# A transfer constant shortened in an instruction planner: accumulating transfers reckoned to land sooner, 70 of them instead of 56, key pairs of the half passes changed, order searched anew

## Chip, core and metric

One core of a Trainium2 chip runs the kernel. The metric is the device time of one execution in microseconds (us), the median over several runs. Engines are named as in the profile: PE (TensorE, matrix products), ACT (ScalarE), DVE (VectorE), POOL (GpSimd), SP (SyncE, which here only issues transfers).

## What is computed

A layer norm, an attention block over it with 32 heads of 20 columns, a token-mixing perceptron over a second layer norm, and a gated sum. S is 2048, D 640, F 1536; all inputs are bf16.

```
xn = layernorm(x)                                   # x: (1, 2048, 640)
q, k, v = split(xn @ wqkv)                          # 32 heads, Dh = 20
p = softmax(q k^T * Dh**-0.5)
s = (p v, heads joined) @ wo
h = layernorm(xn)
u = gelu(einsum("bsd,sf->bdf", h, w1) + b1)         # F = 1536
y = einsum("bdf,fs->bds", u, w2) + b2
out = x + s * silu(y^T)
```

## The kernel before

The instructions of all engines are written by a planner in Python, `_Kern.schedule`, that runs once when the kernel is built. It keeps a clock for each engine (`Prog.T`), adds a reckoned cost for each instruction (`Prog._add`), and always emits next what its own clocks and priorities favour. So a constant of the planner changes no single instruction, but the order of nearly all that come after, and with it who waits for whom.

**Units and passes.** The attention scores are made transposed, in units of 128 keys by 512 queries of one head (L1362, PE). Four heads make a group; 8 groups and 4 query blocks give 32 passes of 64 units, 2048 units in all. The last pass is split into two half passes of 256 queries; there a unit joins two key blocks, named by the list `HP`, of 256 queries each.

**Two ways to the exponential.** Most units go to ACT: PE fills three PSUM banks of one of two bank groups, and one ACT call takes three units (128x1536), or two (128x1024) where the third bank was lent to DVE (L1392, into `pt_sb`). The other units go to DVE, always four heads of one key block together, called a quad here. DVE reads each score tile from PSUM, adds a constant and writes 16-bit integers whose bits are a bf16 power of two (L1403, into `dt_sb`, 128x512, four a quad). Then three more variants of the quad are made, each the first plus a constant, in the bits (L1471, "top", 128x2048, SBUF to SBUF); the four variants are summed with scaled copies of the values (`vs_sb`).

**The accumulating transfer.** A variant can also be made without DVE: POOL issues a transfer from a constant table in DRAM (`kc_scratch_dram`) that adds the constant in place to a variant that isn't needed any more (`emit_x`, L1434, 512 KB). Then a top drops out on DVE. `x_ok` decides on it when a quad has two tops: the reckoned transfer queue must be short, and at least `XLEFT` ACT units of the pass must be left. The transfer waits for the reader of the old variant, on PE (product with the values, L1497) and on DVE (a top); the product with the variant that it makes waits for its landing.

**How the planner reckons it.** On POOL's clock a transfer takes `XISSUE`, then `XMOVE` in a queue of its own, and it is taken as landed `XTAIL` later:

```
if eng == "pool" and ceng != "pool":
    self.T[eng] = start + self.XISSUE
    self.xpipe = max(self.xpipe, start + self.XISSUE) + self.XMOVE
    t.fin = self.xpipe + self.XTAIL
```

With 950, 2900 and 5600 ns that is 9.45 us from the issue to the landing. PE products that need the variant are put in PE's order only behind that time.

**The rest.** Products p v go to one PSUM accumulator (L1497, 32-column pieces of PE side by side); the perceptron and the projections are jobs that PE runs between the score groups (L715 and L723, 32-column and 32-row pieces; L700, L813, L1036); fillers on PE (L1514) add zeros to the accumulator where the planner sees a gap. The weights of the perceptron come in pieces by SP (L850: 1024 KB, L857: 768 KB). ACT also does the gelu (L907) and the tanh of the silu (L920). The residual of most rows is added by POOL's transfers as well (L1078).

**What is searched.** `PLAN` has one string for each stretch of 16 units; a digit chooses a value of one planner option of `OPTS` (slack, priorities, `XLEFT`, and so on) for that stretch.

Of the kernel before, what the change touches and what calls it, by code (L numbers as in the profile page):

```python
# [39 lines left out]
class Prog:  # L40
# [4 lines left out]
    LAT = {"pe": 55.0, "act": 55.0, "dve": 55.0, "pool": 80.0, "sp": 60.0}  # L45
    NXL = 4
    DMAX = 1.4
    XISSUE, XMOVE, XTAIL = 950.0, 2900.0, 5600.0
    TAIL = {"pe": 170.0, "act": 118.0, "dve": 82.0, "pool": 60.0, "sp": 0.0}

    def __init__(self, nc, n_lanes=8):
# [232 lines left out]
class _Kern:  # L284
# [58 lines left out]
    XLEFT, XQ = 20, 4000.0  # L343
# [20 lines left out]
        ("GROT", (1, 0)),  # L364
        ("JOBF", (4, 0, 8)),
        ("EVJ", (36.0, 19.0, 45.0)),
        ("XLEFT", (20, 14, 28, 99)),
        ("XLEFT2", (99,)),
        
        ("NLIVE", (4, 5, 6)),  # L370
        ("D_GUARD", (8, 16, 24)),
    )
    PLAN = (
        "00000000000000000000", "00000000000000000000", "00000000000000000000", "00003000000000000000", "01004000000000000000", "00003000000000000000",
        "00202000000000000000", "00020100000000000000", "10000400000000000000", "00000000000000000000", "00000000001000000000", "00000000000000000000",
        "00000000000000000000", "21004100000000200000", "20100000000000100000", "00000000000000000000", "00000000000000000000", "00204000000000000000",
        "00003000000000000000", "00000000000000000000", "01200000000000000000", "02000030000000000000", "00000000000000000000", "00000000000000000000",
        "00000030000100100000", "00000030000100100000", "01200000000000000000", "02000030000000000000", "10000400000000000000", "20100000000000100000",
        "00003000000000000000", "00000000000000000000", "01000000000000000000", "00000000000000000000", "01000000000000000000", "00000000000000000000",
        "00000000000000000000", "00000000000000000000", "00000000000000000000", "00000000000000100000", "00003000000000000000", "00000000000000000000",  # L380
        "01200000000000000000", "20000000000000000000", "10000000000000000000", "00000000000000000000", "01200000000000000000", "00003000000000000000",
        "00000000000000000000", "00000000000000000000", "10000000000000000000", "10000000000000000000", "00004000001000000000", "00000000000000000000",
        "20020100000000000000", "00000030000100100000", "01003100000000200000", "00000400000000000000", "20000000000000000000", "00000000000000000000",
        "00000000000000000000", "00000000000000000000", "00000000000000000000", "20000000000000000000", "00000000000000000000", "00000000000000000000",
        "00000000000000000000", "02000030000000000000", "20020100000000000000", "00000000000000000000", "00000000000000000000", "00000000000000000000",
        "00000000000000000000", "10000000000000000000", "00000000000000000000", "00000030000100100000", "00000000000000000000", "00000030000100100000",
        "00000000000000000000", "00000000000000000000", "00000000000020000000", "12000000001000000000", "00003000000000000000", "00202000000000000000",
        "00000000000000000000", "00202000000000000000", "00000030000100100000", "00000000000000000000", "20020100000000000000", "00000000000000000000",
        "02000030000000000000", "00000000000000000000", "01003100000000200000", "00000000000000000000", "20020100000000000000", "12000000001000000000",
        "20100000000000100000", "00202000000000000000", "20100000000000100000", "12000000001000000000", "00000030000100100000", "01000000000000000000",  # L390
        "02000030000000000000", "00000000000000000000", "00003000000000000000", "00000000000000000000", "00000000000000000000", "00000000000000000000",
        "01200000000000000000", "00000000000000000000", "00000000000000000000", "01000000000000000000", "00002000000000000000", "00000000000000000000",
        "10000000000000000000", "10000000000000000000", "00000400000000000000", "00000000000000000000", "00020100000000000000", "00000000000000000000",
        "00002000000000000000", "00120100000000100000", "00003000000000000000", "00003000000000000000", "00000000000000000000", "00003000000000000000",
        "00000000000000000000", "00003000000000000000",
    )
    PARTS = (1,)
    DX = (1, 2, 3)
# [78 lines left out]
    def schedule(self):  # L477
# [459 lines left out]
        UP = NB * GH  # L937
        NALL = NG * NTB * UP
        HALF = {NP - 2: 0, NP - 1: 1}
        HP = ((0, 1), (3, 4), (6, 7), (9, 10), (12, 13), (14, 15), (2, 5), (8, 11))  # L940
        units, dunits = [], []
        for q, (G, p) in enumerate(passes):
            if q in HALF:
                a = 256 * HALF[q]
                units.append([[(c0, p * 512 + a, 256, 0, a), (c1, p * 512 + a, 256, 256, a)] for c0, c1 in HP])
                dunits.append([(6, (0, 1)), (7, (2, 3))])
# [1407 lines left out]
```

## Time and profile before

| what | value |
|---|---|
| runs, median (lowest to highest of 3) | 741.89 us (740.93 to 741.89) |
| profiled execution, its own time | 740.37 us |
| its span, first to last instruction | 738.6 us |
| mean granted clock of PE | 0.999 |
| ACT busy | 716.4 us, 97% |
| DVE busy | 705.3 us, 95% |
| PE busy (ends modelled) | 709.1 us, 96% |
| POOL busy | 79.9 us, 11% |

The 1.8 us between the span and the profiled execution's own time lie around the instructions. Three engines are busy for nearly the whole span, so the shares alone don't tell which of them sets the time; the chain of waits and the idle time in front of each group do. In a row of the groups stand line, engine, operation, tiles and shapes, the count, then busy time in us and the mean duration of one in ns, then the engine's idle time in front of them and what ended it. On ACT and DVE instructions overlap: the next one starts some 0.1 to 0.2 us before the last has ended, so the busy time per call is less than the mean duration.

### The profile page before, as it was taken

The numbers are of one execution on the slowest core, as the hardware profiler recorded it, in microseconds if no ns is written. First come the engines' busy times: TensorE is split into PE (matmuls) and PEld (weight loads), VectorE is DVE, ScalarE is ACT, GpSimd is POOL, SyncE is SP. The second block draws the span as 40 slices with busy tenths as digits, with TensorE's granted clock in tenths as the row PEclk, the third lists the DMA queues.
The fourth block names the chain that finished last, engine by engine and source line by source line (L and its number), as shares of the span: only waits on it lengthen the run. The fifth ranks groups of instructions, "written<-read, shape, count | busy, mean of one in ns | idle before, by whom it ended". The sixth has DMA issues, their size and how long they took to land.

```text
span 738.6 us, 23733 instructions
## 1 busy us (share of the span) xinstructions
PE 709.1 (96%) x10544; PEld 237.8 (32%) x10544; DVE 705.3 (95%) x1293; ACT 716.4 (97%) x710; POOL 79.9 (11%) x93
## 2 busy tenths in 40 slices
PE   8899999999999999999999999999999999999997
PEld 6332222222232232322322323232333333233333
DVE  8889999999999999999999999899999999999998
ACT  5999999999999999999999999999999999999995
POOL 4300101010000110000111100111000100121210
PEclk9999999999999999999999999999999999999999
DMA  9768545331444444342644416653368773454333
GB/s 239 146 132 109 103 95 103 69 61 39 95 93 70 84 86 87 80 97 42 146 84 73 80 20 155 125 114 76 83 138 121 116 139 89 88 123 94 63 83 90
DMA packets 132075, 72.56 MB, mean 98 GB/s; under 512 B 84340, under 2 KB 123636, under 8 KB 131924
## 3 DMA queue, kind: packets, MB, share of 16 engines
q1 hardware_dynamic: 122180, 39.71, 25.5%
q0 software_dynamic: 9792, 31.33, 23.6%
q8 instruction: 82, 1.34, 0.8%
q14 instruction: 21, 0.17, 0.1%
HBM read 41.05 MB, written 10.75 MB: 70 GB/s over the span
## 4 chain that ended last, share of the span: by engine, by line
ACT 80%; PE 15%; DVE 2%; DMA 1%; issue 0%; SPq 0%
ACT pt_sb L1392 78%; PE ps_all L1362 5%; PE ps_all L1497 5%; PE ps_all L715 4%; PE ps_all L1036 1%; ACT regB L907 1%; ACT zt_sb L920 1%; DMA regA<-in_A_x_dram 1%; DMA xnT_sb<-regC 1%; DVE dt_sb L1403 1%; DVE dt_sb L1471 0%; DVE bst_sb L596 0%; SPq L541 0%; DVE bst_sb L598 0%; DVE regC L614 0%
## 5 line engine op out<-in xcount | busy, mean ns | idle before, releaser
L1392 ACT ACTIVATE pt_sb<-ps_all 128x1024 bf16<-128x1024 f32 (+1 forms) x681 | 692.8, 1212 | 5.6 <-PE ps_all L1362 4.1
L1403 DVE TENSOR_SCALAR dt_sb<-ps_all 128x512 uint16<-128x512 f32 x536 | 356.1, 683 | 19.3 <-PE ps_all L1362 13.9
L1362 PE MATMUL ps_all<-qk_sb 32*128 32x512 bf16 (+1 forms) x2128 | 268.6, 376 | 17.3 <-ACT pt_sb L1392 15.2
L1471 DVE TENSOR_SCALAR dt_sb<-dt_sb 128x2048 uint16<-128x2048 uint16 x346 | 228.0, 689 | 1.3
L1362 PEld LDWEIGHTS ps_all<-qk_sb 32*128 32x128 bf16 x2128 | 67.9, 91 | 275.4 <-ACT pt_sb L1392 218.2
L1497 PE MATMUL ps_all<-dt_sb,vs_sb 128*21 128x512 bf16 (+1 forms) x1656 | 143.7, 377 | 0.7 <-DVE dt_sb L1471 0.4
L1497 PE MATMUL ps_all<-pt_sb,v_sb 128*21 128x512 bf16 (+1 forms) x1576 | 121.4, 373 | 1.1 <-DVE v_sb L1190 0.8
L1434 POOL DMA_DIRECT2D dt_sb<-kc_scratch_dram x56 | 53.3, 952 | 584.0 <-DVE dt_sb L1471 235.3
L715 PE MATMUL ps_all<-regB,regA 128*32 128x512 bf16 (+1 forms) x1468 | 69.4, 297 | 1.6 <-issue 1.5
L715 PE MATMUL ps_all<-regC,regA 128*32 128x128 bf16 (+1 forms) x1432 | 70.2, 295 | 0.0
L1497 PEld LDWEIGHTS ps_all<-dt_sb,vs_sb 128*21 128x21 bf16 x1656 | 35.8, 90 | 56.3 <-issue 35.9
L1497 PE MATMUL ps_all<-dt_sb,v_sb 128*21 128x512 bf16 (+1 forms) x552 | 52.8, 377 | 0.7 <-DVE tr_sb L1625 0.7
L715 PE MATMUL ps_all<-xnT_sb,wqk_sb 128*32 128x512 bf16 x640 | 48.0, 382 | 0.0
L1497 PEld LDWEIGHTS ps_all<-pt_sb,v_sb 128*21 128x21 bf16 x1576 | 29.2, 90 | 43.3 <-issue 33.4
L723 PE MATMUL ps_all<-regC,regA 32*128 32x512 bf16 x104 | 40.0, 385 | 0.0
L715 PEld LDWEIGHTS ps_all<-regB,regA 128*32 128x32 bf16 x1468 | 29.3, 96 | 25.2 <-issue 13.8
L715 PEld LDWEIGHTS ps_all<-regC,regA 128*32 128x32 bf16 x1432 | 27.6, 96 | 21.2 <-issue 12.7
L1036 PE MATMUL ps_all<-wv_sb,xnT_sb 128*128 128x512 bf16 (+1 forms) x160 | 27.7, 301 | 0.0
L723 PE MATMUL ps_all<-regB,regA 32*128 32x512 bf16 x68 | 26.1, 384 | 0.0
L715 PE MATMUL ps_all<-wv_sb,xnT_sb 128*32 128x480 bf16 x320 | 22.9, 369 | 0.0
L1625 DVE STREAM_TRANSPOSE tr_sb<-ps_all 128x512 f32<-128x512 f32 x31 | 22.0, 710 | 0.0
L1497 PEld LDWEIGHTS ps_all<-dt_sb,v_sb 128*21 128x21 bf16 x552 | 13.9, 90 | 20.9 <-issue 15.8
(88 smaller groups left out, 344.3 us busy)
## 6 DMA issues: line engine op xcount, KB each, us to landing
dt_sb<-kc_scratch_dram POOLq DMA_DIRECT2D x56, 512.0 KB, 6.1
regA<-in_B_w_dram SPq DMA_DIRECT2D x6, 1024.0 KB
regA<-in_B_w_dram SPq DMA_DIRECT2D x8, 768.0 KB
qk_sb<-qk_scratch_dram SPq DMA_DIRECT2D x56, 80.0 KB
qk_scratch_dram<-qs_sb SPq DMA_DIRECT2D x32, 128.0 KB
regA<-in_A_x_dram SPq DMA_DIRECT2D x3, 640.0 KB
ok_scratch_dram<-on_sb SPq DMA_DIRECT2D x96, 20.0 KB
regC<-in_A_x_dram POOLq DMA_DIRECT2D x12, 160.0 KB, 4.1
```

What stands on the lines that cost most here:

```text
L715: fns.append(lambda e, c=c, e_=e_: e.matmul(oc(c, e_), lhsT[:, c:e_], rhs, start=start, stop=stop, tile_position=(0, c)))
L723: row = lambda g: (lambda e: e.matmul(oc(0, 128), lhsT[32 * g:32 * g + 32, :], rhs[32 * g:32 * g + 32, :], start=False, stop=False, tile_p ...
L907: steps.append(("act", lambda e, d=d: e.activation(d, d, AF.Gelu_apprx_tanh), [S_(f"u{f}_{q}") for f in range(f0, f0 + 3) for q in (0, 1)] ...
L920: steps.append(("act", lambda e: e.activation(tt_, z, AF.Tanh), sz, [stt], f"th2_{j}", ac(n)))
L1036: steps.append(("pe", lambda e, c=c: e.matmul(ap, oT_sb[:, c, b * 128:(b + 1) * 128], wo_ap[:, c, c0:c0 + n], start=(opens and c == 0), st ...
L1362: t = pr.pe(lambda e, outp=outp, lhsT=lhsT, rhs=rhs, g=g: e.matmul(outp, lhsT, rhs, start=True, stop=True, tile_position=(32 * g, 0)), rea ...
L1392: tk = pr.act(lambda e: e.activation(outp, inp, AF.Exp, scale=math.log(2.0) / 128.0), reads=[bank_slot[b] for b in banks[:n]], writes=[S_( ...
L1403: tk = pr.dve(lambda e: e.tensor_scalar(w, src, WOFF, 0.0, ALU.add, ALU.max), reads=[bank_slot[bk]], writes=[S_(f"dt{d['tl'][0]}_{g}")], n ...
L1434: t = pr.xdma(lambda e: e.dma_start(dst, src, accum_op=ALU.add), [S_(f"kc{i}")] + sl_, sl_, f"dX{d['q']}_{d['c']}_{k1}")
L1471: tk = pr.dve(lambda e: e.tensor_scalar(dst, src, dk, None, ALU.add), reads=[S_(f"dt{b}_{g}") for b in inb for g in range(4)], writes=[S_( ...
L1497: pr.pe(lambda e: e.matmul(outp, lhsT, rhs, start=(k == 0), stop=last, tile_position=(0, 32 * g)), reads=reads, writes=[bank_slot[AB]], na ...
L1625: steps.append(("dve", lambda e: e.transpose(tr_sb[:, :], ps(AB)), [bank_slot[AB]], [S_("tr")], f"epT{q}", 632.0))
```

## The change

Four edits:

- `XTAIL` goes from 5600 to 4200 ns, so a transfer is taken to land 8.05 us after its issue, not 9.45 us.
- `XLEFT` gets a new first value: 16 units left in the pass are enough for a transfer, where it was 20.
- In the half passes the pairs of key blocks in `HP` change. The two pairs that go to DVE are its last two; they were (2, 5) and (8, 11) and are (1, 4) and (7, 10), which are the first four of the key blocks `RC` of which scaled values exist. The shapes stay.
- `PLAN` is a new table, searched with the new constant.

```diff
-    XISSUE, XMOVE, XTAIL = 950.0, 2900.0, 5600.0
+    XISSUE, XMOVE, XTAIL = 950.0, 2900.0, 4200.0
...
-        ("XLEFT", (20, 14, 28, 99)),
+        ("XLEFT", (16, 20, 14, 28, 99)),
...
     PLAN = (
-        "00000000000000000000", "00000000000000000000", "00000000000000000000", "00003000000000000000", ...
+        "00000000000000000000", "00000000000000000000", "00000000000000000000", "00000000000000000000", ...
...
-        HP = ((0, 1), (3, 4), (6, 7), (9, 10), (12, 13), (14, 15), (2, 5), (8, 11))
+        HP = ((0, 2), (3, 5), (6, 8), (9, 11), (12, 13), (14, 15), (1, 4), (7, 10))
```

What this makes of the instructions, counted in the order of both programs:

| engine, line | before | now |
|---|---|---|
| ACT L1392, two units (128x1024) | 531 | 536 |
| ACT L1392, three units (128x1536) | 150 | 145 |
| ACT L1392, one unit (128x512) | 0 | 1 |
| DVE L1403 (128x512) | 536 | 540 |
| DVE L1471 (128x2048) | 346 | 335 |
| POOL L1434, accumulating transfers | 56 | 70 |
| PE L1497 on `dt_sb`, 512 wide | 2080 | 2096 |
| PE L1497 on `pt_sb`, 512 wide | 1448 | 1444 |
| PE L1514, fillers | 112 | 76 |
| PE L715 / L723 on `regB` (512 wide) | 700 / 68 | 696 / 72 |

All other instructions are the same in kind and number. Up to the first score groups the order is the same on every engine; behind that nearly all rows of PE, ACT and DVE stand otherwise.

POOL's whole queue behind the start, as a piece of the difference (`kc_scratch_dram` is the table of constants; L1078 are the residual's transfers, L1802 clears a weight tile):

```order
-L1434 DMA dt_sb<-kc_scratch_dram 128x2048 x39
+L1434 DMA dt_sb<-kc_scratch_dram 128x2048 x49
 L1802 MEMSET wqk_sb 128x640
-L1434 DMA dt_sb<-kc_scratch_dram 128x2048 x15
+L1434 DMA dt_sb<-kc_scratch_dram 128x2048 x18
 L1078 DMA regC<-in_A_x_dram 128x640 x2
 L1434 DMA dt_sb<-kc_scratch_dram 128x2048
 L1078 DMA regC<-in_A_x_dram 128x640 x4
-L1434 DMA dt_sb<-kc_scratch_dram 128x2048
+L1434 DMA dt_sb<-kc_scratch_dram 128x2048 x2
 L1078 DMA regC<-in_A_x_dram 128x640 x6
```

The added transfers lie in the whole of the attention, ten of them ahead of the clearing of the weight tile, and one among the residual's.

The end of ACT's order before, the last exponentials:

```order
L1392 ACTIVATE pt_sb<-ps_all 128x1536 x2
L1392 ACTIVATE pt_sb<-ps_all 128x1024 x2
L1392 ACTIVATE pt_sb<-ps_all 128x1536
L1392 ACTIVATE pt_sb<-ps_all 128x1024 x5
L1392 ACTIVATE pt_sb<-ps_all 128x1536 x2
L1392 ACTIVATE pt_sb<-ps_all 128x1024
L1392 ACTIVATE pt_sb<-ps_all 128x1536 x2
```

and now:

```order
L1392 ACTIVATE pt_sb<-ps_all 128x1536 x2
L1392 ACTIVATE pt_sb<-ps_all 128x1024
L1392 ACTIVATE pt_sb<-ps_all 128x1536
L1392 ACTIVATE pt_sb<-ps_all 128x1024 x6
L1392 ACTIVATE pt_sb<-ps_all 128x1536 x5
L1392 ACTIVATE pt_sb<-ps_all 128x512
```

The last call takes one unit where it took three, behind five calls of three.

PE's order at the same place before, from the last score group to the end of the last products p v (L1362 scores, L1497 products, L1036 and L1041 the output projection):

```order
L1362 MATMUL ps_all<-qk_sb 128x256 x6
L1497 MATMUL ps_all<-pt_sb,v_sb 21x256 x16
L1497 MATMUL ps_all<-dt_sb,v_sb 21x256 x8
L1497 MATMUL ps_all<-dt_sb,vs_sb 21x256 x16
L1036 MATMUL ps_all<-wv_sb,xnT_sb 128x512
L1041 MATMUL ps_all<-wqk_sb,stage_sb 128x512
L1036 MATMUL ps_all<-wv_sb,xnT_sb 128x512
L1497 MATMUL ps_all<-dt_sb,vs_sb 21x256 x8
L1497 MATMUL ps_all<-pt_sb,v_sb 21x256 x16
```

and now:

```order
L1362 MATMUL ps_all<-qk_sb 128x256 x6
L1497 MATMUL ps_all<-dt_sb,vs_sb 21x256 x8
L1497 MATMUL ps_all<-dt_sb,v_sb 21x256 x8
L1497 MATMUL ps_all<-dt_sb,vs_sb 21x256 x16
L1362 MATMUL ps_all<-qk_sb 128x256 x2
L1497 MATMUL ps_all<-dt_sb,vs_sb 21x256 x8
L1497 MATMUL ps_all<-pt_sb,v_sb 21x256 x16
L1036 MATMUL ps_all<-wv_sb,xnT_sb 128x128 x3
L1497 MATMUL ps_all<-pt_sb,v_sb 21x256 x8
```

The last batch of products holds 8 instead of 16, and a batch of 16 stands ahead of it.

DVE's order from its last score tiles to the transpose of the last half pass before (L1403 score tiles, L1471 tops, L1051 the projection's product with the gate, L1617 to L1622 the close of a half pass):

```order
L1403 TENSOR_SCALAR dt_sb<-ps_all 128x512
L1622 STREAM_TRANSPOSE stage_sb<-on_sb 128x256
L1403 TENSOR_SCALAR dt_sb<-ps_all 128x512
L1471 TENSOR_SCALAR dt_sb<-dt_sb 128x2048 x3
L1051 TENSOR_TENSOR regC<-ps_all,regC 128x512
L1403 TENSOR_SCALAR dt_sb<-ps_all 128x512
L1471 TENSOR_SCALAR dt_sb<-dt_sb 128x2048 x3
L1051 TENSOR_TENSOR regC<-ps_all,regC 128x512
L1617 STREAM_TRANSPOSE tr_sb<-ps_all 128x256
```

and now:

```order
L1403 TENSOR_SCALAR dt_sb<-ps_all 128x512
L1622 STREAM_TRANSPOSE stage_sb<-on_sb 128x256
L1471 TENSOR_SCALAR dt_sb<-dt_sb 128x2048 x2
L1051 TENSOR_TENSOR regC<-ps_all,regC 128x512
L1471 TENSOR_SCALAR dt_sb<-dt_sb 128x2048 x4
L1051 TENSOR_TENSOR regC<-ps_all,regC 128x512
L1617 STREAM_TRANSPOSE tr_sb<-ps_all 128x256
```

Six tops now follow the last score tile, where it was three; the last score tile stands 16 units ahead of ACT's last one, where it was 6.

More of the change, by code (lines that the diff above doesn't have):

```diff
@@ L373 @@
     PLAN = (
[L374 to L393, printed above, removed]
@@ L394 @@
-        "00002000000000000000", "00120100000000100000", "00003000000000000000", "00003000000000000000", "00000000000000000000", "00003000000000000000",
-        "00000000000000000000", "00003000000000000000",
+        "00000000000000000000", "00000000000000000000", "00000000000000000000", "00000000000000000000", "40010000000000000000", "00000000000000000000",
+        "10000400000000000000", "10000400000000000000", "00000000000000000000", "01200000000000000000", "00000000001000000000", "00000000000000000000",
@@ new lines @@
+        "00000000000000000000", "00000030000100100000", "01200000000000000000", "00000000000000100000", "00000100000000000000", "01200000000000000000",
+        "00000000000020000000", "00004000001000000000", "00004000000000000000", "00202000000000000000", "12000000001000000000", "00000100000000000000",
+        "20000000000000000000", "00120100000000100000", "01004000000000000000", "00000100000000000000", "20004100000000000000", "00000000000020000000",
+        "20000000000000000000", "02000030000000000000", "00000000000020000000", "00000400000000000000", "12000000001000000000", "20100000000000100000",
@@ new lines @@
+        "00000000000020000000", "00120100000000100000", "00000000000020000000", "00000000000020000000", "00000000000000000000", "20100000000000100000",
+        "00000000000020000000", "00000000000020000000", "00000000000000000000", "00000000000000000000", "00002000000000000000", "00000000000020000000",
+        "01004000000000000000", "02000030000000000000", "20000000000000000000", "20100000000000100000", "20020100000000000000", "20020100000000000000",
+        "00000000000020000000", "01202000000000000000", "20100000000000100000", "01003100000000200000", "01000000000000000000", "20000000000000000000",
@@ new lines @@
+        "20100000000000100000", "01200000000000000000", "00204000000000000000", "00000000001000000000", "20000000000000000000", "00002000000000000000",
+        "00000030000100100000", "00000400000100000000", "02000000000000000000", "00000030000100100000", "01202000000000000000", "00003000000000000000",
+        "00000000000020000000", "01003100000000200000", "20100000000000100000", "00003000000000000000", "20004100000000000000", "00000000001000000000",
+        "20000000000000000000", "00000000000000000000", "02000030000000000000", "00000000000020000000", "20100000000000100000", "00000000000020000000",
@@ new lines @@
+        "00000030000100100000", "00003000000000000000", "01200000000000000000", "10000000000000000000", "00000000000000000000", "00000000000000000000",
+        "00000000000000000000", "00000000001000000000", "00000000000000000000", "02000030000000000000", "20020100000000000000", "01200000000000000000",
+        "10000000000000000000", "00000000000000000000", "02000030000000000000", "00000000000000000000", "00000000000000000000", "00000000000000000000",
+        "00000000000000000000", "00000000000000000000", "00000000000000000000", "00000000000000000000", "00000000000000000000", "12000000001000000000",
@@ new lines @@
+        "40010000000000000000", "00002000000000000000", "02000000000000000000", "00020100000000000000", "20000000000000000000", "02000000000000000000",
+        "00000000000000100000", "01003100000000200000", "00000000000000000000", "10000000000000000000", "10000400000000000000", "01003100000000200000",
+        "00000000000020000000", "00000100000000000000", "00000000000000000000", "00000000001000000000", "00000000000020000000", "01000000000000000000",
+        "20100000000000100000", "00000000000020000000",
```

## Prediction

> **What bounds the kernel now.** I read the page's shares and its chain of waits first, then ACT by stretches, then who waits for whom.
>
> ```profile
> span 738.6 us, 23733 instructions
> PE 709.1 (96%) x10544; PEld 237.8 (32%) x10544; DVE 705.3 (95%) x1293; ACT 716.4 (97%) x710; POOL 79.9 (11%) x93
> ACT 80%; PE 15%; DVE 2%; DMA 1%; issue 0%; SPq 0%
> ...
> core 0: us, ACT busy (x), PEclk, DMA share, GB/s
> 40.10:437.43 397.33, 396.87 (x397) 1.00 0.44 83
> 437.72:729.91 292.19, 289.68 (x282) 1.00 0.54 106
> 729.91:738.60 8.69, 0.00 (x0) 0.95 0.21 75
> ```
>
> Three engines look full, but 80% of the chain is ACT's. The three stretches (length, then ACT's busy time) say it without a chain: from 40.10 us to its last call at 729.91 us ACT idles 0.46 us in the first and 2.51 us in the second. So the span is a start of 40.10 us, ACT's work, about 3.3 us of its idle time (0.29 us between the stretches included) and an end of 8.69 us. DVE and PE matter only where they let ACT wait, or in that end.
>
> ```profile
> PEld ps_all L1362 <- ACT pt_sb L1392: 218.2, 501, 1.5
> ACT pt_sb L1392 <- PE ps_all L1362: 4.1, 6, 1.1
> PE ps_all L715 <- issue: 1.5, 2, 1.2
> ```
>
> PE's weight loads for the scores waited 501 times for ACT to empty a bank, 0.44 us each; ACT waited for scores six times. PE is thus ahead at nearly every score group. The longest wait of ACT, 1.1 us, stands behind a stall of PE of 1.2 us that no semaphore explains.
>
> **The change, part by part.** ACT first, since it makes the sum.
>
> ```profile
> L1392 ACT ACTIVATE pt_sb<-ps_all 128x1024 bf16<-128x1024 f32 (+1 forms) x681 | 692.8, 1212 | 5.6 <-PE ps_all L1362 4.1 <-PE ps_all L1497 0.5 <-PE ps_all L723 0.3
> ...
> L1392 ACT ACTIVATE pt_sb<-ps_all 128x1024 bf16<-128x1024 f32 x531 | 510.2, 1121 | 2.3 <-PE ps_all L1362 1.4 <-PE ps_all L723 0.3
> L1392 ACT ACTIVATE pt_sb<-ps_all 128x1536 bf16<-128x1536 f32 x150 | 223.8, 1534 | 3.3 <-PE ps_all L1362 2.7 <-PE ps_all L1497 0.5
> ...
> L673 ACT ACTIVATE xnT_sb<-ps_all 128x512 bf16<-128x512 bf16 x2 | 1.2, 597 | 0.7 <-PE ps_all L666 0.6
> ```
>
> Five calls of three units become calls of two: 1534 - 1121 = 413 ns each, 2.07 us less. One call of one unit is new. Calls overlap by 1212 - 692.8/681 = 195 ns; a 128x512 call of 597 ns (L673) so costs 0.40 us, and 1121 - 413 - 195 gives 0.51. I take 0.45, in the middle. **ACT: -1.6 us**, between -1.56 and -1.67, and it lies on the path at full size, because ACT never pauses.
>
> DVE makes one quad more (four L1403) and eleven tops fewer.
>
> ```profile
> L1403 DVE TENSOR_SCALAR dt_sb<-ps_all 128x512 uint16<-128x512 f32 x536 | 356.1, 683 | 19.3 <-PE ps_all L1362 13.9 <-PE ps_all L723 2.8
> L1471 DVE TENSOR_SCALAR dt_sb<-dt_sb 128x2048 uint16<-128x2048 uint16 x346 | 228.0, 689 | 1.3
> ```
>
> 4 x 356.1/536 = 2.7 us more and 11 x 228.0/346 = 7.2 us less: DVE -4.6 us. It is not the bound, so this counts as nothing directly; what covers it is ACT's 99%. It is what pays for the quad: the four units that ACT loses are those that DVE gains.
>
> POOL issues 14 more transfers.
>
> ```profile
> L1434 POOL DMA_DIRECT2D dt_sb<-kc_scratch_dram x56: 872/875/1635, 63.5 to 696.7; - x56
> DMA to landing us min/median/max: 4.9/6.1/11.0
> L1471 DVE TENSOR_SCALAR dt_sb<-dt_sb x346: 631/689/832, 44.2 to 728.5; 128x2048 uint16<-128x2048 uint16 x173
> ```
>
> 14 x 0.875 = 12 us on an engine that is busy for 79.9 of 738.6 us; the data is 14 x 512 KB, and the DMA engines are 44% and 54% busy in the two stretches. Both are covered. What an issue costs DVE is bounded by the tops: none took over 832 ns where the median is 689, so at most 14 x 0.14 = 2.0 us, at least nothing; I take nothing, since the 4.6 us that DVE gains cover either end. [...]
>
> On PE 36 fillers go, 16 pieces of products on `dt_sb` come and 4 on `pt_sb` go.
>
> ```profile
> L1497 PE MATMUL ps_all<-dt_sb,vs_sb 128*21 128x512 bf16 (+1 forms) x1656 | 143.7, 377 | 0.7 <-DVE dt_sb L1471 0.4
> L1497 PE MATMUL ps_all<-pt_sb,v_sb 128*21 128x512 bf16 (+1 forms) x1576 | 121.4, 373 | 1.1 <-DVE v_sb L1190 0.8
> L1514 PE MATMUL ps_all<-wp_sb,zw_sb 128*21 128x512 bf16 (+1 forms) x112 | 8.9, 374 | 0.0
> ```
>
> 16 x 143.7/1656 - 4 x 121.4/1576 = +1.1 us of work against 36 x 8.9/112 = 2.9 us of filler: nothing, covered by the 0.44 us that PE waits for ACT at a score group. If that cover were gone, 1.1 us would count. The fillers stood where PE had nothing to do, so their going frees no time; that the granted clock stays at 1.00 without them is an assumption.
>
> The pairs of the half passes keep their shapes, 256 wide in both kernels: nothing. The end: behind ACT's last call PE has this to do.
>
> ```profile
> 730.25 0.41 PE L1497 MATMUL ps_all<-dt_sb,vs_sb 128*21 128x256 bf16 x8
> 730.47 0.62 PE L1497 MATMUL ps_all<-pt_sb,v_sb 128*21 128x256 bf16 x16
> 731.16 0.45 DVE L1617 STREAM_TRANSPOSE tr_sb<-ps_all 128x256 f32<-128x256 f32 x1 [0.33 <-PE ps_all L1497]
> ```
>
> The transpose of DVE waits for the last product. With 8 instead of 16 in the last batch it comes 0.62 - 0.41 = 0.2 us sooner; at worst the three short projection pieces now ahead of it take that back, so between 0 and -0.2, and I take **-0.2 us** since PE can run those pieces while ACT is still at its last call.
>
> **The wait that the change tightens.** Each product that needs a transferred variant may stand 1.4 us nearer to the issue: counted in the order by the semaphores, between what lets a transfer go and its first use ACT gets 14 to 41 units before, median 25, and 11 to 37 now, median 22. On PE everything behind a late product waits too, the next scores first, and ACT behind them. Two landings of before were long:
>
> ```profile
> L1434 POOL DMA_DIRECT2D dt_sb<-kc_scratch_dram x1: 1182/1182/1182, 208.2 to 208.2; - x1
> DMA to landing us min/median/max: 11.0/11.0/11.0
> ...
> L1434 POOL DMA_DIRECT2D dt_sb<-kc_scratch_dram x1: 872/872/872, 358.8 to 358.8; - x1
> DMA to landing us min/median/max: 10.5/10.5/10.5
> ...
> 207.97 0.44 SPq L850 DMA_DIRECT2D regA<-in_B_w_dram  x1
> 358.40 0.40 SPq L850 DMA_DIRECT2D regA<-in_B_w_dram  x1
> ```
>
> Both were issued within 0.4 us behind a weight piece of 1024 KB from SP, and queued behind it. Their first uses had 30 and 28 units of distance, and no engine waited for a transfer of this kind. Now, by the same count, one transfer goes two ACT calls, about 2 us, behind such a piece and has 18 units of distance, 18 x 692.8/1512 = 8.2 us (1512 units in ACT's 692.8 us), against a landing of some 11.0 - 2.0 = 9 us: 0.8 us late. Four more go within three calls of a piece, with 19 to 21 units, just in time. ACT has one call in hand, about 1.0 us (692.8/681), so the likeliest cost is 0. [...]
>
> **The sum.** -1.6 - 0.2 = -1.8 us. The profiled execution took 740.37 us, 1.8 us more than its span, so it would now take 738.6. The median of the runs is 741.89 us; the same step from there gives **740.1 us**, 0.24% less. About 0.2%, 1.5 us, is what a measurement of this kernel can tell from no change.
>
> **Rivals.**
>
> A, the forecast: ACT's work shrinks, its idle time stays. 739.3 to 740.9 us by its own range, from half the end's gain and 0.7 us more or less of idle time.
>
> B, ACT waits more: heavy PE stretches fall elsewhere in the new order, where ACT has no call in hand. For it: 2.5 of its 3.3 us of idle time lie in the second stretch, where the perceptron's second half is fitted in. Against it: PE's work between score groups grows by only 1.1 us in all. If that idle time doubles, -1.8 + 2.5 = +0.7: 742.6 us.
>
> C, late transfers, the other side: a transfer behind a weight piece lands 11.0 us after its issue where the planner now reckons 8.05; less the call in hand, (11.0 - 8.05) - 1.0 = 2.0 us each. Two such make -1.8 + 4.0 = +2.2, 744.1 us; it decides from two on (slower by 0.2% needs 3.3 us lost). For it: transfers are 25% more, pieces as many. Against it: a 6.1 us median, and PE's 0.44 us of slack at each group to catch up.
>
> D, more gained: the 2.5 us of idle time, with the unexplained 1.2 us stall in it, mostly goes because DVE is freer. -1.8 - 1.8: 738.3 us.
>
> E, the change does nothing: the end eats what ACT saves, because six tops stand behind DVE's last score tile where it was three, 3 x 228.0/346 = 2.0 us more: -1.8 + 2.0, 742.1 us. Against it: ACT has 16 units to do behind that tile, where it was 6, and 10 x 692.8/1512 = 4.6 us cover the 2.0.
>
> **How the numbers follow.** A 0.45 (0.31 of it below 740.4 us, 0.14 within 0.2%), B 0.22 (0.17 within, 0.05 slower), C 0.12 (0.09 slower, 0.03 within), D 0.15, E 0.06. That gives faster 0.46, same 0.40, slower 0.14. The point is A's. The range goes from D's 738.3 to 742.8, just past B, and leaves out the far part of C and what D may gain beyond.
>
> **What would show it.** ACT's calls in the groups: 536 and 145 with about 691.2 us in all; between its first and last call about 3 us of idle time; DVE busy near 700.7 us; POOL's L1434 70 times with a median landing near 6.1 us. Products on `dt_sb` waiting for a transfer, in PE's list of waits, would show C; ACT waiting for scores for more than 5 us would show B. A granted clock below 1.00 in the body, or an end longer than 8.7 us, would make the sum wrong.

## The result and the profile after

The changed kernel took **745.69 us** (median of 11 runs, 742.48 to 752.59) against 740.93 us for the kernel before on the same chip (11 runs, 740.33 to 744.55): a ratio of 1.0063, 95% interval 1.0037 to 1.009. A second comparison on another chip gave 742.96 against 739.89 us, 1.0052 (1.0028 to 1.0077). It is slower by half a per cent, where 740.1 us was forecast. The profiled execution took 746.19 us.

The page's span, its busy times and the engines' shares of the chain of waits:

```profile
span 744.4 us, 23686 instructions
PE 709.4 (95%) x10506; PEld 236.9 (32%) x10520; DVE 701.0 (94%) x1286; ACT 715.5 (96%) x711; POOL 91.5 (12%) x107
ACT 69%; PE 17%; DMA 6%; DVE 6%; issue 1%; SPq 0%; DVEq 0%
```

ACT works 0.9 us less and the span is 5.8 us longer: the loss is idle time. Its share of the chain falls from 80% to 69%, and DMA has 6% where it had 1%. The span by stretches, with ACT's busy time and the granted clock of TensorE, shows where:

```profile
40.10:205.00 164.90, 164.75 (x164) 1.00 0.49 88
205.00:225.00 20.00, 16.30 (x17) 0.91 0.54 110
225.00:369.00 144.00, 143.03 (x144) 1.00 0.54 101
369.00:377.00 8.00, 5.17 (x6) 0.79 0.36 107
377.00:736.15 359.15, 356.96 (x353) 1.00 0.56 109
736.15:744.40 8.25, 0.00 (x0) 0.94 0.24 83
```

Two short stretches, 28 us in all, hold 3.70 + 2.83 = 6.5 us of ACT's 9.8 us of idle time. The other three hold 3.3 us, as much as the whole body had before (1.6 us of it is lost to two further late transfers, named below). The same two stretches are the only ones in the body where the clock is below 1.00. The waits say what came ahead of the first:

```profile
PEld ps_all L1362 <- ACT pt_sb L1392: 222.7, 513, 1.0
...
ACT pt_sb L1392 <- PE ps_all L1362: 9.4, 12, 2.6
...
PEld ps_all L1497 <- DMA dt_sb<-kc_scratch_dram: 5.6, 3, 3.1
...
PE ps_all L1497 <- DMA dt_sb<-kc_scratch_dram: 4.5, 3, 2.6
...
PE ps_all L715 <- issue: 1.5, 1, 1.5
```

Products now wait for a transferred variant, three times, 4.5 us in all and 2.6 us at the longest; before there was no such row. ACT waits 9.4 us for scores where it was 4.1. The timeline around the longest wait (start, length, engine and line, and in brackets the idle time ahead of the instruction):

```profile
201.59 12.98 ACT L1392 ACTIVATE pt_sb<-ps_all 128x1536 bf16<-128x1536 f32 x12
...
205.42 0.44 SPq L850 DMA_DIRECT2D regA<-in_B_w_dram  x1
205.58 0.87 POOL L1434 DMA_DIRECT2D dt_sb<-kc_scratch_dram  x1 [16.92 <-PE ps_all L1497]
...
213.19 0.60 PE L1497 MATMUL ps_all<-pt_sb,v_sb 128*21 128x512 bf16 x8
...
216.44 0.40 PE L1497 MATMUL ps_all<-dt_sb,vs_sb 128*21 128x512 bf16 x4 [2.65 <-DMA dt_sb<-kc_scratch_dram]
...
217.19 2.10 ACT L1392 ACTIVATE pt_sb<-ps_all 128x1024 bf16<-128x1024 f32 x2 [2.63 <-PE ps_all L1362]
...
217.63 0.60 PE L1362 MATMUL ps_all<-qk_sb 32*128 32x512 bf16 x3
```

SP issues a weight piece of 1024 KB at 205.42 us, POOL a transfer 0.16 us later, and that transfer takes 10.8 us. PE reaches its product at 216.44 - 2.65 = 213.8 us, 8.2 us behind the issue, and stands. ACT loses 2.63 of those 2.65 us. Then a group of scores takes 0.60 us where it takes 0.39 us elsewhere: the granted clock is 0.50 for 3.41 us from 217.68 us on, and ACT pauses twice more, 0.95 us. The other two late transfers, issued at 319.2 and 596.0 us behind pieces of 317.5 and 592.3 us, landed after 9.3 and 9.2 us and held PE for 1.1 and 0.7 us and ACT for 0.9 and 0.7 us, without a half-clock window. The second window, at 371.3 us with 0.50 for 3.41 us, stands behind the stall of 1.5 us on L715 that no semaphore explains; with it ACT loses 2.8 us. The kernel before has a stall of this kind too, of 1.2 us, with no half clock behind it.

What the change did to the work itself, in the groups:

```profile
L1392 ACT ACTIVATE pt_sb<-ps_all 128x1024 bf16<-128x1024 f32 (+1 forms) x682 | 692.1, 1210 | 12.0 <-PE ps_all L1362 9.4 <-PE ps_all L723 1.6 <-PE ps_all L1497 0.5
L1403 DVE TENSOR_SCALAR dt_sb<-ps_all 128x512 uint16<-128x512 f32 x540 | 357.3, 680 | 24.6 <-PE ps_all L1362 16.3 <-PE ps_all L723 6.3
L1471 DVE TENSOR_SCALAR dt_sb<-dt_sb 128x2048 uint16<-128x2048 uint16 x335 | 222.3, 685 | 3.9 <-PE ps_all L1497 2.8
```

And the transfers' issues on POOL (shortest, median and longest in ns), with their landings:

```profile
L1434 POOL DMA_DIRECT2D dt_sb<-kc_scratch_dram x70: 872/872/1420, 64.9 to 703.2; - x70
DMA to landing us min/median/max: 4.9/6.3/11.2
```

The longest, 11.2 us, is the transfer issued right behind the late one, at 207.95 us; nothing waited for it.

### The profile page after: what moved, and what is told of

Read it like the earlier page. It is cut to its first block, busy times and chain, and to the rows that moved or that the text cites. A ratio compares the mean times of both kernels' runs of the same rounds, so it can differ in the third digit from the quotient of the medians.

```text
span 744.4 us, 23686 instructions
## 1 busy us (share of the span) xinstructions
PE 709.4 (95%) x10506; PEld 236.9 (32%) x10520; DVE 701.0 (94%) x1286; ACT 715.5 (96%) x711; POOL 91.5 (12%) x107
## 4 chain that ended last, share of the span: by engine, by line
ACT 69%; PE 17%; DMA 6%; DVE 6%; issue 1%; SPq 0%; DVEq 0%
ACT pt_sb L1392 67%; PE ps_all L1497 5%; PE ps_all L1362 5%; DMA dt_sb<-kc_scratch_dram 4%; PE ps_all L715 4%; DVE dt_sb L1403 2%; PE ps_all L1036 1%; ACT zt_sb L920 1%; ACT regB L907 1%; DMA regA<-in_A_x_dram 1%; DVE dt_sb L1471 1%; DMA xnT_sb<-oT_scratch_dram 1%; DMA xnT_sb<-regC 1%; DMA oT_scratch_dram<-stage_sb 1%; DVE bst_sb L596 0%
## 5 line engine op out<-in xcount | busy, mean ns | idle before, releaser
L1392 ACT ACTIVATE pt_sb<-ps_all 128x1024 bf16<-128x1024 f32 (+1 forms) x682 | 692.1, 1210 | 12.0 <-PE ps_all L1362 9.4
L1403 DVE TENSOR_SCALAR dt_sb<-ps_all 128x512 uint16<-128x512 f32 x540 | 357.3, 680 | 24.6 <-PE ps_all L1362 16.3
L1362 PE MATMUL ps_all<-qk_sb 32*128 32x512 bf16 (+1 forms) x2128 | 269.5, 377 | 15.1 <-ACT pt_sb L1392 13.7
L1471 DVE TENSOR_SCALAR dt_sb<-dt_sb 128x2048 uint16<-128x2048 uint16 x335 | 222.3, 685 | 3.9 <-PE ps_all L1497 2.8
L1362 PEld LDWEIGHTS ps_all<-qk_sb 32*128 32x128 bf16 x2128 | 68.0, 91 | 274.2 <-ACT pt_sb L1392 222.7
L1497 PE MATMUL ps_all<-dt_sb,vs_sb 128*21 128x512 bf16 (+1 forms) x1668 | 144.0, 379 | 4.8 <-DMA dt_sb<-kc_scratch_dram 4.5
L1434 POOL DMA_DIRECT2D dt_sb<-kc_scratch_dram x70 | 64.9, 928 | 576.6 <-PE ps_all L1497 248.4
L1497 PE MATMUL ps_all<-pt_sb,v_sb 128*21 128x512 bf16 (+1 forms) x1572 | 120.6, 375 | 1.4 <-DVE v_sb L1190 0.8
L715 PE MATMUL ps_all<-regC,regA 128*32 128x128 bf16 (+1 forms) x1432 | 69.9, 296 | 1.5 <-issue 1.5
L715 PE MATMUL ps_all<-regB,regA 128*32 128x512 bf16 (+1 forms) x1464 | 65.7, 297 | 1.1 <-DVE qs_sb L765 0.6
L1497 PEld LDWEIGHTS ps_all<-dt_sb,vs_sb 128*21 128x21 bf16 x1668 | 36.1, 90 | 63.3 <-issue 39.7
L1497 PE MATMUL ps_all<-dt_sb,v_sb 128*21 128x512 bf16 (+1 forms) x556 | 53.3, 378 | 0.1
L715 PE MATMUL ps_all<-xnT_sb,wqk_sb 128*32 128x512 bf16 x640 | 48.9, 383 | 0.2 <-DVE v_sb L1190 0.2
L1497 PEld LDWEIGHTS ps_all<-pt_sb,v_sb 128*21 128x21 bf16 x1572 | 28.4, 91 | 42.7 <-issue 33.2
L723 PE MATMUL ps_all<-regC,regA 32*128 32x512 bf16 x104 | 40.4, 388 | 0.0
L715 PEld LDWEIGHTS ps_all<-regC,regA 128*32 128x32 bf16 x1432 | 27.6, 96 | 23.8 <-issue 14.6
L715 PEld LDWEIGHTS ps_all<-regB,regA 128*32 128x32 bf16 x1464 | 27.1, 96 | 25.1 <-issue 12.9
L723 PE MATMUL ps_all<-regB,regA 32*128 32x512 bf16 x72 | 27.7, 384 | 0.0
L1036 PE MATMUL ps_all<-wv_sb,xnT_sb 128*128 128x128 bf16 (+1 forms) x148 | 25.0, 294 | 2.4 <-issue 0.9
L715 PE MATMUL ps_all<-wv_sb,xnT_sb 128*32 128x480 bf16 x320 | 21.8, 369 | 0.0
L1497 PEld LDWEIGHTS ps_all<-dt_sb,v_sb 128*21 128x21 bf16 x556 | 13.7, 90 | 20.2 <-issue 16.0
```

The costliest lines, as they stand in the source:

```text
L715: fns.append(lambda e, c=c, e_=e_: e.matmul(oc(c, e_), lhsT[:, c:e_], rhs, start=start, stop=stop, tile_position=(0, c)))
L723: row = lambda g: (lambda e: e.matmul(oc(0, 128), lhsT[32 * g:32 * g + 32, :], rhs[32 * g:32 * g + 32, :], start=False, stop=False, tile_p ...
L1036: steps.append(("pe", lambda e, c=c: e.matmul(ap, oT_sb[:, c, b * 128:(b + 1) * 128], wo_ap[:, c, c0:c0 + n], start=(opens and c == 0), st ...
L1362: t = pr.pe(lambda e, outp=outp, lhsT=lhsT, rhs=rhs, g=g: e.matmul(outp, lhsT, rhs, start=True, stop=True, tile_position=(32 * g, 0)), rea ...
L1392: tk = pr.act(lambda e: e.activation(outp, inp, AF.Exp, scale=math.log(2.0) / 128.0), reads=[bank_slot[b] for b in banks[:n]], writes=[S_( ...
L1403: tk = pr.dve(lambda e: e.tensor_scalar(w, src, WOFF, 0.0, ALU.add, ALU.max), reads=[bank_slot[bk]], writes=[S_(f"dt{d['tl'][0]}_{g}")], n ...
```

## Experiments

Theory L: late transfers behind weight pieces stall PE, ACT has nothing in hand, and the clock adds to a long stall. Its rivals: the new order itself (O), the traffic as such (T). Each ratio is to the kernel before, run beside it on the same chip. The edits are shown in outline. Line numbers of edited kernels stand a few lines further down; what the line does is said.

**Small weight pieces (w_small).**

```diff
-src = B_w1[:, k * 256:(k + 1) * 256]...     # 16 row blocks, 1024 KB
+if k >= 2: src = B_w1[0:256, ...]           # 2 row blocks, 128 KB; w2 likewise
```

> The changed kernel, the same order on every engine, but the weight pieces that SP loads in the flow (from the third piece of each half on) move 128 KB instead of 1024 KB; it leaves out loading most of the perceptron's weights. Theory L (late transfers: three accumulating transfers queue behind such a piece, PE and then ACT stand for them, and the granted clock halves after the longest stall): the landings near 11 us go, PE waits for no transfer for more than 1 us in all, ACT's idle time between its first and last call falls from 20.7 us in all to about 14 us, and the time falls by 4 to 6 us to 739.5 to 741.5 us. Rival O (the new order itself: heavy stretches of PE fall where ACT has no call in hand): the three waits for transfers go from the list but ACT's idle time stays near 20 us and the time within 1.5 us of the changed kernel's 745.7 us.

Measured: 737.63 us, ratio 0.996 (0.9944 to 0.9975). Landing of the transfers, and the stretch in which ACT had lost 3.70 us:

```profile
DMA to landing us min/median/max: 4.7/6.0/8.6
```

```profile
205.00:225.00 20.00, 20.00 (x22) 1.00 0.37 65
```

No engine waits for an accumulating transfer, ACT is full in this stretch and the clock stays at 1.00. With the order untouched the loss is gone and the kernel is 2.5 us faster than before, 1.9 us below the range that L expected. O falls.

**Half transfers (x_half).**

```diff
-dst = dt_sb[:, b0, :, :]
+dst = dt_sb[:, b0, 0:2, :]
```

> The changed kernel, the same order on every engine, but each accumulating transfer moves half of its columns (256 KB instead of 512 KB); it leaves out the addition for two of the four heads of each transferred variant. The weight pieces are whole. Theory L: the median landing falls from 6.3 us to 4 to 5 us and those behind a weight piece from about 11 us to 7 to 9 us, the waits of PE for transfers (4.5 us on products, 5.6 us on weight loads) fall below 2 us, and the time falls by 3 to 6 us to 739.5 to 742.5 us. Rival O: time within 1.5 us of 745.7 us, ACT's idle time unchanged.

Measured: 736.77 us, ratio 0.9953 (0.9936 to 0.997), 2.7 us below the expected range. What is left of the waits for a transfer, and the landings:

```profile
PEld ps_all L1497 <- DMA dt_sb<-kc_scratch_dram: 0.7, 1, 0.7
PE ps_all L1497 <- DMA dt_sb<-kc_scratch_dram: 0.2, 1, 0.2
```

```profile
DMA to landing us min/median/max: 3.4/4.5/8.4
```

The other partner of the collision was halved, and the effect is the same. The slowest landings, 8.3 and 8.4 us, are again those of the two transfers at the piece of 205 us, issued at 205.1 and 207.5 us; the median is 4.5 us. How two queues share the way there was not shown.

**Later issues in the kernel before (b_late).**

```diff
+e.tensor_tensor(dl_sb[:, c:c + 12], ..., ALU.pow)   # POOL, 2.5 us in this run, ahead of each transfer
 return e.dma_start(dst, src, accum_op=ALU.add)
```

> The kernel before, the same order on every engine, with an idle small power on POOL (12 elements, about 2 us) in front of each accumulating transfer, so that each is issued some 2 us later than its semaphores allow; POOL has room for 56 x 2 us. Theory L holds that it is the margin of the single transfer that counts: in the kernel before, six of the 56 transfers land 0.1 to 2.3 us ahead of their first use, the others earlier, so a few waits of 0.5 to 2 us appear, and with the granted clock's half windows behind them 1 to 5 us more than before: 742 to 746 us. Rival O, for which transfers do not matter: within 1 us of 740.9 us. If the time grows by far more than 5 us, POOL's slower issue costs something other than the margin.

Measured: 750.23 us, ratio 1.014 (1.0117 to 1.0164).

```profile
PEld ps_all L1503 <- DMA dt_sb<-kc_scratch_dram: 8.2, 3, 4.6
PE ps_all L1503 <- DMA dt_sb<-kc_scratch_dram: 7.1, 3, 4.3
```

L1503 is the line of the products. In the order of the kernel before, later transfers alone make the loss. As in the changed kernel only three of them come late, but the time is 4 us beyond the expected upper end: the longest wait is 4.3 us and half-clock time of 6.83 us begins in it. The two longer waits, 4.3 and 1.9 us, are for transfers issued 1.6 and 0.8 us behind a weight piece, which landed after 11.8 and 10.0 us; the third, 0.9 us at 70 us, stands behind no such piece.

**The old constant under the new table (xtail_old), the new constant alone (xtail_only).**

```diff
 # xtail_old, from the changed kernel        # xtail_only, from the kernel before
-XTAIL = 4200.0                              -XTAIL = 5600.0
+XTAIL = 5600.0                              +XTAIL = 4200.0
```

> The changed kernel with the transfer constant back at 5600, and its own order table, pairs and the first value of the other table kept; the planner then writes another order, with 64 transfers. Theory L: with 1.4 us more reckoned for each transfer PE waits for transfers less than 2 us in all, and the time is 739 to 742 us unless the table, which was searched for the other constant, leaves ACT idle elsewhere. Rival O: the table and the pairs carry the loss, and the time stays at 744 to 747 us without waits for transfers.

> The kernel before with the transfer constant 4200 alone; its order table, pairs and XLEFT of 20 stay. The planner then writes another order with 55 transfers. Theory L: the constant lets transfers come late as in the changed kernel, so waits of PE for transfers of 2 us or more appear; and a table that was searched for the other constant no longer fits, as the run with the old constant and the new table showed: 745 to 760 us. Rival: the constant alone hardly changes what the planner does, and the time is 739 to 743 us.

Measured: 758.94 us, ratio 1.0255 (1.0234 to 1.0276), and 771.09 us, 1.0428 (1.0413 to 1.0443), each beyond every range that was expected. Of the first, busy times:

```profile
PE 717.4 (95%) x10580; PEld 243.0 (32%) x10580; DVE 681.7 (90%) x1250; ACT 725.0 (96%) x705; POOL 87.6 (12%) x101
```

Of the second:

```profile
PE 723.7 (94%) x10608; PEld 242.6 (32%) x10608; DVE 694.9 (90%) x1273; ACT 723.3 (94%) x705; POOL 79.0 (10%) x92
```

Both give ACT 7 to 9 us more to do than the kernel before (716.4 us), because DVE gets 516 and 524 score tiles instead of 536 and 540. That is less than half of their loss; ACT's waits for products, 7.0 and 10.8 us (0.5 us before), are another part, and the rest was not taken apart. xtail_old has one wait for a transfer, 0.2 us on a weight load; xtail_only has 5.5 us of them on products. So neither the constant nor the table can be judged alone: each did worse without the other. The pairs of the half passes were not tried alone. These two runs do not separate the parts of the change and bear on L only by the presence and absence of the waits.

**Weight pieces in quarters (a_trickle on the changed kernel, b_trickle on the one before).**

```diff
-pr.dma(load of the whole piece, writes=wr)
+for a in range(0, blocks, blocks // 4):      # each waits for the one before to land
+    pr.dma(load of rows a to a + blocks // 4, writes=wr)
```

> The changed kernel, the same order on every compute engine and the same bytes, but each weight piece in the flow (from the third of each half on) goes as four pieces of a quarter, each of which SP issues only when the one before has landed. Theory L (an accumulating transfer queues behind a whole piece of 1024 KB): landings near 11 us fall to 7 to 8 us, PE's waits for transfers fall below 1.5 us in all, and the time is 736.5 to 738.5 us, as with the small pieces. Rival T (what helped with small pieces and half transfers was the smaller traffic as such): the bytes are the same, so the time stays at 743 to 747 us.

> The kernel before with the same quartered weight pieces. Theory L: no transfer of it was waited for, so nothing is gained: 739.5 to 741.5 us, within 0.2% of before. Then the change, with its late transfers cured, is worth the difference between this run and the changed kernel's with quartered pieces, forecast as -1.8 us, measured with small pieces as about -2.5. Rival T: as the traffic is smoothed, before gains 2 to 4 us as well.

Measured: 747.01 us, ratio 1.01 (1.0083 to 1.0117), and 746.2 us, 1.0087 (1.0074 to 1.01): both outside what L expected. The first stands at the edge of where T had put it, but its waits show another reason (L715 computes with the weights, L1379 are scores, L1409 is ACT's exponential; the landings follow):

```profile
ACT pt_sb L1409 <- PE ps_all L1379: 11.6, 8, 7.4
PE ps_all L715 <- DMA regA<-in_B_w_dram: 5.7, 1, 5.7
```

```profile
DMA to landing us min/median/max: 4.6/6.1/8.8
```

No wait for an accumulating transfer is left, as L said. But the last piece of the second half, stretched to a chain of four, now lands too late: PE stands 5.7 us for it until 635.7 us, ACT 7.4 us, and half-clock time comes with it (a granted clock of 0.70 from 630 to 640 us). The kernel before has the same new wait of 6.0 us. So the edit cures one wait and makes another.

**Stalls put in on purpose (b_stall).**

```diff
+pool: m memsets of 128x512, behind this score group      # m = 1, 2, 3, 4, 5, 2, 3
+pe:   the next instruction waits for them
```

> The kernel before, with seven stalls of PE put in, about 85 us apart: PE waits there for 1, 2, 3, 4, 5, 2 and 3 memsets on POOL of some 0.5 us each, so about 0.8, 1.3, 1.8, 2.3, 2.8, 1.3 and 1.8 us. Theory L with the clock (a stall costs its length less the call that ACT has in hand, and from about 1.5 us on a window of 3.41 us at half clock, some 1.7 us more): half-clock windows behind the four stalls of 1.8 us and more, about 5 us for the stalls and 7 us for the windows, 750 to 754 us. Rival N (the windows come on their own and not from stalls): the clock stays at 1.00 behind them, 744 to 747 us.

Measured: 762.1 us, ratio 1.0312 (1.0294 to 1.033), 8 us above L's upper end. Three of the seven stalls in the timeline (L1373 is the memset) and what ACT lost behind each:

```profile
202.29 0.40 PE L1509 MATMUL ps_all<-dt_sb,v_sb 128*21 128x512 bf16 x4 [1.26 <-POOL dl_sb L1373]
203.27 1.02 ACT L1404 ACTIVATE pt_sb<-ps_all 128x1024 bf16<-128x1024 f32 x1 [1.01 <-PE ps_all L1365]
...
282.15 0.39 PE L1365 MATMUL ps_all<-qk_sb 32*128 32x512 bf16 x1 [1.81 <-POOL dl_sb L1373]
283.44 1.02 ACT L1404 ACTIVATE pt_sb<-ps_all 128x1024 bf16<-128x1024 f32 x1 [1.97 <-PE ps_all L1365]
...
533.21 0.60 PE L1365 MATMUL ps_all<-qk_sb 32*128 32x512 bf16 x1 [1.49 <-POOL dl_sb L1373]
535.36 1.02 ACT L1404 ACTIVATE pt_sb<-ps_all 128x1024 bf16<-128x1024 f32 x1 [2.47 <-PE ps_all L1365]
```

Stretches of the same kernel (length, PE, PEld, DVE, ACT and POOL busy, clock):

```profile
203.30:206.71 3.41, 3.16 (x81) 1.29 (x73) 3.34 (x8) 3.41 (x4) 0.00 (x0) 1.00 0.02 5
283.99:287.40 3.41, 3.41 (x30) 0.83 (x31) 2.62 (x5) 2.50 (x3) 0.00 (x0) 0.50 0.30 96
...
533.16:539.99 6.83, 6.78 (x108) 2.79 (x109) 4.01 (x8) 3.55 (x4) 0.00 (x0) 0.50 0.22 44
```

The stalls of 0.64 and 1.26 us have no half-clock window. The five of 1.49, 1.81, 1.81, 2.60 and 3.01 us have one each, in the stall or just behind it, of 3.41 us three times and 6.83 us twice. ACT loses 1.01 us of the stall of 1.26 and more than the whole of the longer ones: next to nothing in hand covers a stall. The seven stalls sum to 12.6 us and the time grows by 22.5 us, which leaves about 10 us for seven half-clock periods of 3.41 us, an estimated 1.4 us each if every stall costs its length.

But length alone does not decide whether a window follows. Three stalls longer than 1.49 us have no half clock behind them: 1.52 us in a_trickle (at 707.5 us), 1.90 us in b_late (at 600.7 us) and 2.86 us in xtail_old (at 419.5 us). In the changed kernel and in b_stall the half-clock windows of the trace start whole multiples of 3.41 us apart: the changed kernel's two, at 217.68 and 371.30 us, 45 such steps, and those of b_stall, at 283.99, 362.49, 441.00, 533.16 and 621.90 us, 23, 23, 27 and 26. Counted on in such steps from a window of the same trace, the steps around five stalls are these (length, PE busy, clock): two of b_stall with a window behind them, then a_trickle, b_late and xtail_old.

```profile
280.58:283.99 3.41, 1.84 (x23) 1.00 0.35 85
618.49:621.90 3.41, 1.88 (x40) 1.00 0.07 20
...
705.66:709.08 3.42, 1.90 (x27) 1.00 0.87 163
...
598.49:601.91 3.42, 2.19 (x30) 1.00 1.28 143
601.91:605.32 3.41, 2.74 (x43) 1.00 0.92 187
...
417.57:420.98 3.41, 1.95 (x29) 1.00 1.08 244
420.98:424.40 3.42, 2.02 (x31) 1.00 1.10 253
```

PE idles 1.57 and 1.53 us of the step ahead of the window in these two cases of b_stall, and 2.17 and 1.54 us ahead of the changed kernel's two, where no other step of the body has more than 1.14 us; ahead of b_stall's other three windows the stall itself takes 2.47, 1.37 and 1.44 us of the step. The three stalls without a window leave at most 1.52 us of idle time in a step; two of them fall across the border of two steps. xtail_only does not fit: two of its three windows stand behind steps with 1.3 and 1.0 us of idle time, and a step with 1.6 us has none. So this is a reading of the traces afterwards, and no run was made to test it.

**The late pieces alone in quarters (a_one: the piece of 205 us; a_three: those of 205, 317 and 592 us), and all but the last (a_most, b_most).**

> The changed kernel with one weight piece alone in quarters, each issued when the one before has landed: the third of the first half, behind which the longest wait stood (issued at 205.4 us). Theory L with prices from the changed kernel's trace: ACT's idle time of 2.63, 0.48 and 0.47 us at 217.2 to 221.3 us goes, 3.6 us, and nothing else: 745.7 - 3.6 = 742.1, between 741 and 743.5 us, and no half-clock window near 217 us. Rival (the late transfer only moves to the next piece, or the windows come on their own): 744 to 747 us.

> The changed kernel with the three weight pieces in quarters behind which PE waited for a transfer (issued at 205.4, 317.5 and 592.3 us), all others whole. Theory L: 3.6 us at 217, 0.9 us at 329 and 0.7 us at 606 us go, 5.2 us: 740.5 us if the stall of PE at 370 us, which no semaphore explains, stays with its 2.8 us of ACT's idle time, and 737.7 us if it goes too. Rival: above 743 us.

> The changed kernel with all weight pieces of the flow in quarters but the last of the second half, which stays whole since the chain of four made it land too late (PE waited 5.7 us for it and ACT 7.4). Theory L: no wait for a transfer above 1 us, no late weight piece, no half-clock window before the end: 746.5 (the run with all in quarters, against 739.6 of before) less 7.4 and less the window behind it, 737 to 738.5 us, faster than before. Rival: another quartered piece or a stored row that SP now issues later is waited for instead, 740 to 744 us.

> The kernel before with the same pieces in quarters, the last one whole. Theory L: the 7.5 us wait for the last piece goes, and nothing else was waited for: within 0.2% of before, 738.5 to 740.5 us. The difference between this kernel and the changed one with the same pieces is the change without late transfers: about -1.8 to -2.5 us. Rival (the queue's traffic as such costs before something too): 736 to 738 us, and the change is then worth nothing.

Measured, against 739.63 us of before beside them: a_one 740.97 us, ratio 1.001 (0.9993 to 1.0026); a_three **737.64 us, 0.997 (0.9957 to 0.9983)**; a_most 739.09 us, 0.9985 (0.9971 to 0.9998); b_most 740.25 us, 1.0006 (0.9991 to 1.002). By the first comparison's ratio the changed kernel would stand at 739.63 x 1.0063 = 744.3 us here: one piece gives back 3.3 of the 3.6 us that were expected of it, by the second comparison's 1.0052 it is 2.5. Three pieces give 6.7 or 5.8, expected were 5.2 or 8.0. The stretches of a_three:

```profile
205.00:225.00 20.00, 20.00 (x22) 1.00 0.52 110
...
361.00:369.00 8.00, 7.02 (x8) 1.00 0.55 132
```

Its exponentials, on a line 17 further down:

```profile
L1409 ACT ACTIVATE pt_sb<-ps_all 128x1024 bf16<-128x1024 f32 (+1 forms) x682 | 691.2, 1216 | 5.0 <-PE ps_all L1379 3.5 <-PE ps_all L1514 0.5 <-PE ps_all L723 0.5
```

In the first stretch nothing is left of the loss. The stall without a semaphore is there in the second, with 1.0 us, and no window follows it. a_most came out 1.5 us above a_three, where no difference was expected; its trace shows PE waiting 1.3 us for rows of the output projection (0.4 in a_three), and five of its twelve runs, the five slowest, have a mean clock of 0.997 or 0.998; what starts the half clock in them is in no trace. In a_three the bytes are those of the changed kernel and the loss is gone, and b_most shows that quartered pieces do nothing for the kernel before, as L expects. T falls.

**The changed kernel and a_one once more, for their traces (after2, a_one2).**

> The changed kernel once more, beside the next. If the half-clock window at 371 us is a chance of the instruction stream (a stall of PE between 1.0 and 1.5 us that no semaphore explains) and the one at 217.7 us belongs to the late transfer, the second is in every execution and the first in some: granted clock 0.998 in some runs and 0.995 in others, never 1.000, 743 to 748 us.

> The changed kernel with the first late weight piece in quarters, for its trace. Theory L: PE does not stall near 210 us and there is no window there; the waits for the transfers behind the pieces of 317 and 592 us (1.4 and 1.0 us) stay; the stall at about 364 to 366 us is there with 1.0 to 1.6 us, and a half-clock window behind it only if it is longer than the 1.26 us that had none among the stalls put in on purpose. Time 739 to 743 us.

after2 took 742.96 us, and its profiled execution has the window behind the late transfer (a stall of 2.06 us, half clock at 217.20 us) and none at 371 us; its runs had a mean clock of 0.998 to 0.993, none 1.000. a_one2 took 739.83 us, in one run; its waits for transfers (L1514 are the products) are those of the two other pieces:

```profile
PEld ps_all L1514 <- DMA dt_sb<-kc_scratch_dram: 2.7, 2, 1.6
PE ps_all L1514 <- DMA dt_sb<-kc_scratch_dram: 2.1, 2, 1.3
```

No half-clock window stands in its body. The window of 217 us therefore belongs to the late transfer. That of 371 us comes with a stall which the traces of this order show with 0.3 to 1.5 us or not at all; where it comes from was not settled.

## Why the prediction was wrong

**The step that failed** is "so the likeliest cost is 0" in the part on the wait that the change tightens. It had three terms. The transfer of 205.58 us fits the one named there. The distance was right: 18 units were put at 8.2 us, and PE came 8.2 us behind the issue. The landing was not: the order showed the transfer two ACT calls behind the weight piece, so 11.0 - 2.0 = 9 us were taken; in the run SP issued the piece 0.16 us ahead of the transfer and the landing took 10.8 us. The 11.0 us was right, the 2.0 us taken off it was not: SP's place in the order did not give its time. The third term was worst: a call in hand of 1.0 us. ACT lost 2.63 us of a stall of 2.65, and in b_stall 1.01 us of the stall of 1.26 and more than the whole of the longer ones. It did run on for 0.8 us when PE stopped at 213.8 us, until its call ended at 214.57; but from PE's restart at 216.44 to ACT's next call at 217.19, behind a batch of products and the scores, it takes as long, so nothing is left to cover a stall. PE's wait of 0.44 us at each score group shows that PE is ahead of ACT by a part of one group, not that ACT has a finished group in store. Two more transfers came late, where four more had been called just in time. So the term that was put at 0 cost 5.1 us of ACT's idle time in the profiled execution: 2.63, 0.89 and 0.67 us behind the three stalls and 0.95 us of half clock. The 2.8 us at 371 us come on top; no step of the prediction bears on them. after2, without them, is still 3.1 us slower than before.

**Rival C** was the case that happened. It gave 744.1 us for two late transfers of 2.0 us; there were three, of 2.6, 1.1 and 0.7 us, and their sum is close to its 4.0. What C lacked is the half-clock window, 1 us of ACT behind the first, and the stall at 371 us. "A granted clock below 1.00 in the body" was named as what would make the sum wrong, for another reason: the fillers. Without the 36 fillers a_three and a_one2 have no half clock in their bodies, so those were not missed.

**The sum held where it could be seen apart.** ACT's exponentials fell from 692.8 us to 692.1 in the changed kernel and to 691.2, the forecast figure, in a_three. DVE 701.0 us (700.7 forecast), POOL 70 transfers at a median of 6.3 us (6.1), the end 8.25 us, 0.4 less (0.2). a_three is 2.0 us faster than before, where the sum said 1.8.

**B and E did not happen.** The sign named for B, ACT waiting for scores for more than 5 us, did show with 9.4 us, but late transfers, the stall at 371 us and their half clock make it as well, so it could not tell B from C; with the order untouched and those waits gone, w_small has 3.7 us. E's end is shorter, not longer. **D** is not clearly seen: a_three gains 2.0 us, near A's 1.8 and not D's 3.6; w_small (2.5 us) and x_half (3.4 us) come nearer, but they move fewer bytes.

## What to carry to other kernels

A transfer constant of 8.05 us, above the median landing of 6.3, was still too short where a big transfer on another queue can stand ahead: take the landing behind that piece (10.8 us here), or split the piece that stands ahead of a tight transfer, and only that one, since a split piece comes later itself (PE waited 5.7 us for the last one in a_trickle). Before a wait is called covered, show that the engine at the bound has finished work in store; here a stall of PE reached ACT almost in full (2.63 of 2.65 us). A stall is to be priced with the clock behind it (another 0.95 us of ACT's time here), and a table searched for one constant could not be kept here when the constant was changed.

## What the runs showed of the hardware that was not expected

Stalls of TensorE of 1.49 to 3.01 us were followed by half clock for 3.41 or 6.83 us in the changed kernel and in b_stall, those of 1.26 us and less were not; but neither were stalls of 1.52, 1.90 and 2.86 us in three other runs. The half-clock windows of the changed kernel and of b_stall start whole multiples of 3.41 us apart in their traces. How a stall falls on these steps fits better than its length in four cases with a window (1.53 to 2.17 us of PE's idle time in the step ahead) and three without (at most 1.52 us), but not in xtail_only. A stall of 1.81 us had one period behind it, one of 1.49 us two (3.41 and 6.83 us). A transfer of 512 KB issued 0.16 us behind a piece of 1024 KB on another queue took 10.8 us instead of 6.3, and those of 256 KB at the same piece still 8.3 and 8.4 instead of 4.5: about 4 us more in either size.
